# Attention visits ahead of an expert layer: sums inverted a visit sooner, transposes and copies issued ahead of exponents, other counts of constant products

## The chip, the cores and the metric

The kernel runs on one core of a Trainium2 chip. The metric is device time in microseconds (us), the median of the runs; 884.2 us for the kernel before, from three runs between 883.71 and 885.02. A lower time is better.

## The reference

Windowed attention over 8 batches, 8 heads, 576 positions and 64 elements a head, followed by an expert layer on all 4608 tokens.

```python
scores = scale * np.matmul(q, k.transpose(0, 1, 3, 2))
scores = np.where(masks[None, :, :, :], scores, -1000000000.0)   # 32 keys, or every 4th of 128
attn = np.exp(scores - np.max(scores, axis=-1, keepdims=True))
attn = attn / (np.sum(attn, axis=-1, keepdims=True) + 1e-09)
x = np.matmul(attn, v).transpose(0, 2, 1, 3).reshape(B * S, H * D)
h = x @ w_in                      # 4608 x 512 by 512 x 2048
sp = np.maximum(h, 0.0) + np.log1p(np.exp(-np.abs(h)))
out = (h * erf(sp)) @ w_out       # 2048 x 512
```

The weights come as double-precision words; the kernel makes of each a high and a low part on the chip.

## The kernel before

**Units and visits.** The attention is cut into 72 units of four blocks of 64 queries, for two heads at once. Unit n is begun at visit n and ended at visit n + 3 (LAG = 3). A visit is one pass of `first_visit(n)` (L366), of which the first 14 (FIRST = 14, n = 0 to 13) run ahead of the first product of the expert layer; later visits are woven into the steps of that layer (from L1342). Below, m = n - 3 is the unit that a visit ends.

**The steps of a unit**, with the engine and line of each: scores (TensorE, 32 small products, L224); the mask with the row maximum (VectorE, four instructions, L235); exponents with their row sums (ScalarE, four instructions, L245); 1e-9 added to the sums (POOL, L250); the reciprocal of the sums (VectorE, L257) and the multiplication of the probabilities by it (POOL, L258), together `normalize`; two transposes (TensorE, L263); a copy of the transposed probabilities from PSUM to SBUF, `turned` (L267, on ScalarE or VectorE); values (TensorE, 32 small products, L282); row copies out of PSUM (ScalarE, L324). When a pair of heads is complete, `finish` splits its rows into a high part (ScalarE, L329) and a low part (VectorE, `part_lo`, L335).

**The weights.** Visits 1 to 9 (EARLY = 9) also prepare weights: `prep_act` on ScalarE (L446 casts the high part of a tile made in the visit before, L451 begins the next tile), `prep_dve` on VectorE behind the visit (L460 the low part, L464 to L466 shift and combine the words of the tile that ScalarE began a visit earlier). At its end `prep_dve` issues the load of a further tile into the buffer that has come free (L431, 512 KB).

**The queues.** The order of instructions on every engine is the order in which the program issues them. All loads are issued on SP: q and k of unit n + 2 behind the scores of visit n (L208, 272 or 288 KB, two buffers, free when the scores two units before are done), v of unit n - 1 at the end of visit n (L212, 256 KB, two buffers, free when the values of unit n - 3 are done), and the weights tile at the end of `prep_dve`. So SP's order in a visit is q and k, v, weights.

**The visit before.** TensorE has transposes of m, scores of n, constant products, values of m, constant products. The constant products (`busy`, L364) multiply a constant tile into a PSUM bank that nobody reads until the first real product overwrites it; a visit that ends a unit has two behind the scores and two behind the values, the others six behind the scores. VectorE has `normalize(n - 2)`, then the mask of n, then the low parts, then the weights. ScalarE has the copy for unit m (visits 3 to 9; VectorE has it in visits 10 to 13), the weights, the row copies, the high part, the exponents of n. POOL has the multiplication for unit n - 2, then the addition for unit n. Behind the last visit `normalize(FIRST - 2)` follows, then the first step of the expert layer: transposes of unit 11 and the first product (L528).

Of the kernel before, what the change touches and what calls it, by code (L numbers as in the profile page):

```python
# [66 lines left out]
FIRST = NBLK + LAG + 2  # L67
# [3 lines left out]
EARLY = 9  # L71
# [75 lines left out]
def attn_moe_kernel(ctx: ExitStack, tc: tile.TileContext, qk, v, masks, eye, w_in, w_out, out):  # L147
    nc = tc.nc
# [47 lines left out]
    def turn_place(u):  # L196

        return (acc[(u + 1) % 4] if u < FREE else spb[u in second])[:, PARTS * P:2 * PARTS * P]
# [6 lines left out]
    def load_qk(u):  # L205
        if u < NU:
            n = QW + key_start(u, SPU - 1) + KEYS
            nc.sync.dma_start(out=qkz[u % 2][:, 0:n], in_=qk[u, :, 0:n])  # L208

    def load_v(u):  # L210
        if has(u):
            nc.sync.dma_start(out=vz[u % 2], in_=v[u].rearrange("p (s h d) -> p s h d", s=SIDE, h=2))  # L212
# [28 lines left out]
    def exponents(u):  # L241
        nmax = maxes.pop(u)
        sums[u] = small.tile([P, 2 * PARTS], F32, name="ssum", bufs=LAG + 1)
        for j in range(2 * PARTS):
            nc.scalar.activation(  # L245
                out=probs[u][:, j, :], in_=probs[u][:, j, :], func=AF.Exp,
                scale=-1.0, bias=nmax[:, j:j + 1], accum_out=sums[u][:, j:j + 1],
            )
        if u < FIRST:
            nc.gpsimd.tensor_scalar(sums[u], sums[u], 1.0e-9, None, op0=ALU.add)  # L250

    def normalize(u):
        rinv = small.tile([P, 2 * PARTS], F32, name="rinv")

        if u >= FIRST:
            nc.vector.tensor_scalar(sums[u], sums[u], 1.0e-9, None, op0=ALU.add)  # L256
        nc.vector.reciprocal(out=rinv, in_=sums.pop(u))  # L257
        nc.gpsimd.tensor_tensor(probs[u], probs[u], rinv.broadcast_to([P, 2 * PARTS, KEYS]), op=ALU.mult)  # L258

    def transposes(u):  # L260
        pr = probs.pop(u)
        for h in range(2):
            nc.tensor.transpose(out=turn_place(u)[:, h * P:(h + 1) * P],  # L263
                                in_=pr[:, PARTS * h:PARTS * (h + 1), :].rearrange("p a k -> p (a k)"), identity=ident)

    def turned(u, copy):
        copy(out=pz[u in second][:, 0:2 * P], in_=turn_place(u))  # L267
# [54 lines left out]
    def rows(u):  # L322
        for to, src in rows_of(u):
            nc.scalar.copy(out=to, in_=src)  # L324
# [7 lines left out]
    def part_lo():  # L332
        while halved:
            hi, lo, src = halved.pop(0)
            nc.vector.tensor_tensor(out=lo, in0=src, in1=hi.bitcast(F32), op=ALU.subtract)  # L335
# [20 lines left out]
    def has(u):  # L356
        return 0 <= u < NU
# [3 lines left out]
    def busy(k):  # L361

        for _ in range(k):
            nc.tensor.matmul(h, idle[:, 0:P], idle, start=True, stop=True)  # L364

    def first_visit(n):  # L366

        m = n - LAG
        copy = nc.scalar.copy if 1 <= n <= EARLY else nc.vector.tensor_copy
        if has(m):  # L370
            transposes(m)
        scores(n)
        load_qk(n + 2)
        busy(2 if has(m) else 6)
        if has(m):
            turned(m, copy)
        if 1 <= n <= EARLY:
            prep_act()
        if has(m):
            values(m)  # L380
            busy(2)
        if has(n - 2):
            normalize(n - 2)
        mask_max(n)
        part_lo()
        if has(m):
            rows(m)
            finish(m)
        if m == NBLK - 1:
            part_lo()  # L390
        exponents(n)
        load_v(n - 1)

# [920 lines left out]
    with tc.manual_schedule():  # L1314
# [6 lines left out]
        for n in range(FIRST):  # L1321
# [2 lines left out]
            first_visit(n)  # L1324
            if 1 <= n <= EARLY:
                prep_dve()
        normalize(FIRST - 2)
        part_lo()

        plan, late = visits()  # L1330
# [196 lines left out]
```

## Time and profile before

| what | value |
|---|---|
| median of three runs | 884.2 us |
| the profiled execution's own time | 884.02 us |
| its span, first to last instruction | 882.2 us |
| granted TensorE clock, mean | 0.998 |
| TensorE busy | 98% of the span |
| VectorE, ScalarE, POOL busy | 79%, 69%, 9% |
| first visit's scores start | 4.65 us |
| first product of the expert layer starts | 49.26 us |

The span is what the profile covers, 1.8 us less than the execution's own time. A row of a timeline tells when an instruction ran and, in brackets, how long its engine had been idle and what ended that. A share over the whole span is an average over stages: the first 49 us, which the diff touches, have other limits than the rest, where TensorE is busy nearly all the time. The granted clock is the share of full speed (2.4 GHz) at which TensorE was let run.

### The profile page before, as it was taken

What the parts mean: (1) busy time and instruction counts of PE and PEld (TensorE: products, weight loads), DVE (VectorE), ACT (ScalarE), POOL (GpSimd) and SP (SyncE); (2) the same over time, 40 slices, a digit from 0 to 9 for tenths busy, and PEclk for the clock granted to TensorE, in tenths of its full rate; (3) what the DMA queues carried; (4) which work ended last, traced back from release to release, by engine and by line L of the source; (5) the groups of instructions that cost most, each with busy time, mean ns of one, the idle gap of its engine ahead of it and who ended that gap; (6) DMA issues with size and microseconds to landing.
All of it is one profiled execution on the core that took longest, in us unless ns stands there. A gap on an engine that the chain in (4) does not pass through costs nothing.

```text
span 882.2 us, 21971 instructions
## 1 busy us (share of the span) xinstructions
PE 861.0 (98%) x8410; PEld 709.1 (80%) x8422; DVE 696.2 (79%) x1766; ACT 608.2 (69%) x1364; POOL 79.7 (9%) x97
## 2 busy tenths in 40 slices
PE   7689999999999999999999999999999999999998
PEld 3467888888888888888888888888888888889998
DVE  5888888987688889877766875667887968888985
ACT  6889888897797886675677652774656547785441
POOL 2312201111111100001000100000000000000000
PEclk9999999999999999999999999999999999999999
DMA  8874446474558797667576843674688449999332
GB/s 279 293 252 153 138 146 199 141 239 131 182 211 277 272 312 300 206 200 254 183 231 223 285 168 107 207 245 169 201 261 299 169 143 323 333 338 366 127 121 65
DMA packets 83161, 193.03 MB, mean 219 GB/s; under 512 B 9072, under 2 KB 25712, under 8 KB 79984
## 3 DMA queue, kind: packets, MB, share of 16 engines
q1 hardware_dynamic: 80096, 183.17, 61.6%
q10 hardware_dynamic: 2960, 8.46, 2.4%
q8 instruction: 66, 1.08, 0.5%
q14 instruction: 39, 0.32, 0.1%
HBM read 133.92 MB, written 57.67 MB: 217 GB/s over the span
## 4 chain that ended last, share of the span: by engine, by line
PE 90%; DMA 3%; ACT 3%; DVE 2%; issue 1%; POOL 0%; SPq 0%; DVEq 0%; POOLq 0%
PE acc L643 32%; PE h L803 10%; PE tx L803 10%; PE h L528 7%; PE tx L528 7%; PE sp L803 6%; PE acc L1166 4%; PE sp L282 3%; PE sp L224 3%; PE sp L1166 3%; PE sp L263 1%; DMA dbl<-in_w_in_dram 1%; PE tx L1166 1%; PE h L1166 1%; ACT prob L245 1%
## 5 line engine op out<-in xcount | busy, mean ns | idle before, releaser
L643 PE MATMUL acc<-wout_hi,ghi 128*128 128x512 f32 x448 | 177.4, 396 | 0.0
L643 PE MATMUL acc<-wout_lo,ghi 128*128 128x512 f32 x448 | 174.7, 390 | 0.0
L643 PE MATMUL acc<-wout_hi,glo 128*128 128x512 f32 x448 | 123.9, 390 | 0.2 <-DVE glo L619 0.2
L258 POOL TENSOR_TENSOR prob<-prob,rinv 128x256 f32<-128x256 f32 x72 | 71.5, 1001 | 473.2 <-DVE ssum L256 237.5
L245 ACT ACTIVATE prob<-prob,nmax 128x64 f32<-128x64 f32 x288 | 96.3, 338 | 10.5 <-DVE nmax L235 10.3
L643 PEld LDWEIGHTS acc<-wout_hi,glo 128*128 128x128 f32 x448 | 84.0, 188 | 18.4 <-DVE glo L619 0.6
L643 PEld LDWEIGHTS acc<-wout_hi,ghi 128*128 128x128 f32 x448 | 84.2, 188 | 17.0 <-DVE ghi L618 0.4
L643 PEld LDWEIGHTS acc<-wout_lo,ghi 128*128 128x128 f32 x448 | 84.2, 188 | 16.7
L235 DVE CUSTOM_DVE_ANT_0 prob<-sp,cst 128x64 f32<-128x64 f32 x288 | 45.2, 220 | 37.1 <-ACT rows L324 25.9
L852 ACT ACT_TABLE_LOAD x26 | 33.4, 1283 | 48.9 <-DVE hc L820 24.6
L803 PE MATMUL tx<-win 128*128 128x512 f32 x216 | 55.9, 394 | 0.0
L803 PE MATMUL h<-win 128*128 128x512 f32 x216 | 55.8, 394 | 0.0
L245 ACT ACTIVATION_READ_ACCUMULATOR prob<-prob,nmax 128x1 f32 x288 | 54.6, 190 | 0.0
L528 PE MATMUL h<-x,win 128*128 128x512 f32 x192 | 48.8, 396 | 0.0
L528 PE MATMUL tx<-x,win 128*128 128x512 f32 x192 | 48.0, 392 | 0.0
L803 PEld LDWEIGHTS h<-win 128*128 128x128 f32 x216 | 39.9, 188 | 9.3 <-DVE dbl L822 0.7
L803 PEld LDWEIGHTS tx<-win 128*128 128x128 f32 x216 | 39.9, 188 | 9.1 <-DVE hc L822 0.3
L324 ACT COPY rows<-sp 128x128 f32<-128x128 f32 (+7 forms) x167 | 27.5, 308 | 27.2 <-PE sp L224 26.8
L852 ACT ACTIVATE s<-dbl 128x1024 f32<-128x1024 f32 x22 | 23.3, 1061 | 27.4 <-DVE dbl L820 27.3
L528 PEld LDWEIGHTS h<-x,win 128*128 128x128 f32 x192 | 35.4, 188 | 8.0
L528 PEld LDWEIGHTS tx<-x,win 128*128 128x128 f32 x192 | 35.7, 188 | 7.5
L282 PEld LDWEIGHTS sp<-pT,v 64*64 64x64 f32 x1824 | 29.3, 134 | 10.6 <-DVE s L612 4.6
(338 smaller groups left out, 1938.5 us busy)
## 6 DMA issues: line engine op xcount, KB each, us to landing
win<-ws SPq DMA_DIRECT2D x24, 1024.0 KB, 5.3
v<-in_v_dram SPq DMA_DIRECT2D x72, 256.0 KB, 4.7
win<-ws SPq DMA_DIRECT2D x24, 768.0 KB, 6.0
qk<-in_qk_dram SPq DMA_DIRECT2D x48, 272.0 KB, 5.0
dbl<-in_w_in_dram SPq DMA_DIRECT2D x16, 512.0 KB, 4.4
dbl<-in_w_out_dram SPq DMA_DIRECT2D x16, 512.0 KB, 4.0
ws<-x SPq DMA_DIRECT2D x32, 256.0 KB, 4.3
win<-wd SPq DMA_DIRECT2D x14, 512.0 KB, 8.8
```

The source lines that it names most:

```text
L224: nc.tensor.matmul(sps[h][r * STRIP:(r + 1) * STRIP, i, p, :], qkz[i][hs, s * STRIP:(s + 1) * STRIP], qkz[i][hs, at:at + KEYS], start=True ...
L235: nc.vector.tensor_tensor_reduce(out=pr[:, g, :], in0=sps[h][:, u % 2, p, :], in1=mask[QUADS.index(kinds(u, p))], scale=-SCALE, scalar=HUG ...
L245: nc.scalar.activation(out=probs[u][:, j, :], in_=probs[u][:, j, :], func=AF.Exp, scale=-1.0, bias=nmax[:, j:j + 1], accum_out=sums[u][:, ...
L258: nc.gpsimd.tensor_tensor(probs[u], probs[u], rinv.broadcast_to([P, 2 * PARTS, KEYS]), op=ALU.mult)
L263: nc.tensor.transpose(out=turn_place(u)[:, h * P:(h + 1) * P], in_=pr[:, PARTS * h:PARTS * (h + 1), :].rearrange("p a k -> p (a k)"), iden ...
L282: nc.tensor.matmul(xp[h * D:(h + 1) * D, qs], vt[ks, s, h, :], pt[ks, h * P + s * STRIP:h * P + (s + 1) * STRIP], start=True, stop=True, t ...
L324: nc.scalar.copy(out=to, in_=src)
L528: nc.tensor.matmul((h, bank)[j], win_at[:, ftp, j, cc // 2, w, cc % 2, :], x[cc], start=(k == 0 and i == 0), stop=(k == CC - 1 and i == 2))
L643: nc.tensor.matmul(args["out"], args["lhsT"], args["rhs"], start=args["start"], stop=args["stop"])
L803: nc.tensor.matmul(bank_, w[:, wi, c, :], x[c][:, xi, :], start=(c == 0 and n == 0), stop=(c == 1 and n == 2))
L852: nc.scalar.activation(out=l, in_=e, func=AF.Softplus)
L1166: nc.tensor.matmul(y, x[:, at_], w, start=(q == 0 and j == 0 and n == 0), stop=(q == QUART - 1 and j == 1 and n == 2))
```

## The change

- `normalize` moves within the visit: for unit n - 1 behind the mask of n and the row copies, instead of for unit n - 2 ahead of the mask of n. On VectorE the reciprocal thereby stands ahead of the weights of the same visit. `normalize(FIRST - 2)` behind the last visit is dropped, as visit 13 contains it.
- The transposes of unit m + 1 and the copy of them stand at the end of visit n, ahead of the exponents of n, instead of at the head of visit n + 1. The first are in visit 2; visit 13 has none, as the first step of the expert layer transposes unit 11 as before. The copy is on ScalarE in visits 2 to 9 (units 0 to 7, one more than before) and on VectorE in visits 10 to 12 (units 8 to 10).
- Constant products: three behind the scores and three behind the values in visits 3 to 10, one and one in visits 11 to 13. Visits 0 to 2 keep their six.

```diff
--- before.py
+++ after.py
@@ -366,21 +366,14 @@
     def first_visit(n):
 
         m = n - LAG
-        copy = nc.scalar.copy if 1 <= n <= EARLY else nc.vector.tensor_copy
-        if has(m):
-            transposes(m)
         scores(n)
         load_qk(n + 2)
-        busy(2 if has(m) else 6)
-        if has(m):
-            turned(m, copy)
+        busy(6 if not has(m) else 3 if n <= EARLY + 1 else 1)
         if 1 <= n <= EARLY:
             prep_act()
         if has(m):
             values(m)
-            busy(2)
-        if has(n - 2):
-            normalize(n - 2)
+            busy(3 if n <= EARLY + 1 else 1)
         mask_max(n)
         part_lo()
         if has(m):
@@ -388,6 +381,11 @@
             finish(m)
         if m == NBLK - 1:
             part_lo()
+        if has(n - 1):
+            normalize(n - 1)
+        if has(m + 1) and n + 1 < FIRST:
+            transposes(m + 1)
+            turned(m + 1, nc.scalar.copy if n <= EARLY else nc.vector.tensor_copy)
         exponents(n)
         load_v(n - 1)
 
@@ -1324,7 +1322,6 @@
             first_visit(n)
             if 1 <= n <= EARLY:
                 prep_dve()
-        normalize(FIRST - 2)
         part_lo()
 
         plan, late = visits()
```

## Rows read from the trace of the kernel before

**Rows 1.** The page, part 1, for the whole span: busy us of each engine (share of the span) and x its instructions.

```profile
PE 861.0 (98%) x8410; PEld 709.1 (80%) x8422; DVE 696.2 (79%) x1766; ACT 608.2 (69%) x1364; POOL 79.7 (9%) x97
```

**Rows 2.** The chain of waits that ended last, in order of time: start us, us, what.

```profile
36.27 5.58 DMA v<-in_v_dram
...
45.00 0.42 DVE pT L267
...
45.79 0.22 POOL ssum L250
...
46.09 0.62 POOL prob L258
...
46.76 0.44 PE acc L263 x2
```

**Rows 3.** The timeline of TensorE (PE): start us, us, engine, line, operation, output<-inputs, x merged, and in brackets the idle time before it with what ended it. L263 are transposes, L364 constant products, L224 scores, L282 values, L528 the first products of the expert layer. Some records of L364 are missing.

```profile
11.62 0.38 PE L263 MATMUL acc<-ident,prob 128*128 128x128 f32 x2
...
25.89 1.04 PE L364 MATMUL h<-plain 128*128 128x512 bf16 x2
...
41.34 0.46 PE L224 MATMUL sp<-qk 64*32 64x64 f32 x32 [0.27 <-DMA qk<-in_qk_dram]
41.96 0.38 PE L364 MATMUL h<-plain 128*128 128x512 bf16 x1 [0.16 <-DMA v<-in_v_dram]
42.27 0.67 PE L282 MATMUL acc<-pT,v 64*64 64x32 f32 x32
42.87 0.60 PE L364 MATMUL h<-plain 128*128 128x512 bf16 x2
...
45.48 0.67 PE L282 MATMUL acc<-pT,v 64*64 64x32 f32 x32 [0.57 <-DVE pT L267]
...
49.09 0.41 PE L263 MATMUL acc<-ident,prob 128*128 128x128 f32 x2
49.26 3.02 PE L528 MATMUL h<-x,win 128*128 128x512 f32 x12
...
61.03 0.67 PE L282 MATMUL acc<-pT,v 64*64 64x32 f32 x32 [0.52 <-DMA v<-in_v_dram]
...
71.20 0.41 PE L263 MATMUL sp<-ident,prob 128*128 128x128 f32 x2 [1.13 <-DVE nmax L235]
```

**Rows 4.** The table of stretches: from:to in us, length, then busy us (x instructions) of TensorE, of its weight loads, of VectorE, ScalarE and POOL, the granted TensorE clock as a share of full speed, the busy share of the DMA engines, GB/s.

```profile
11.07:38.70 27.63, 19.28 (x522) 10.96 (x528) 25.63 (x98) 25.41 (x107) 8.23 (x14) 0.94 0.90 298
38.80:49.26 10.46, 8.23 (x244) 4.86 (x247) 5.51 (x43) 6.95 (x39) 3.86 (x8) 1.00 0.86 261
21.00:24.50 3.50, 1.56 (x36) 0.77 (x36) 3.28 (x14) 2.86 (x14) 0.15 (x1) 1.00 0.96 316
24.90:28.30 3.40, 3.07 (x69) 1.92 (x70) 2.52 (x8) 3.33 (x14) 1.94 (x4) 0.50 0.83 302
49.26:71.20 21.94, 19.45 (x324) 14.84 (x324) 20.26 (x65) 19.76 (x53) 5.74 (x9) 1.00 0.82 273
```

**Rows 5.** DMA issues of the v loads in four short windows, in order: the loads issued at 32.84 (unit 7), 36.27 (unit 8), 39.61 (unit 9) and 43.02 us (unit 10). Columns: output<-input, queue, operation, x issues, KB each, median us from issue to landing.

```profile
v<-in_v_dram SPq DMA_DIRECT2D x1, 256.0 KB, 4.3
...
v<-in_v_dram SPq DMA_DIRECT2D x1, 256.0 KB, 5.6
...
v<-in_v_dram SPq DMA_DIRECT2D x1, 256.0 KB, 4.8
...
v<-in_v_dram SPq DMA_DIRECT2D x1, 256.0 KB, 3.8
```

**Rows 6.** The timeline of VectorE (DVE), columns as in rows 3. L460 is the subtraction of a weights tile, L464 its shift, L465 and L466 its two combining steps, L267 the copy of transposed probabilities.

```profile
20.00 0.69 DVE L460 TENSOR_TENSOR win<-w,win 128x512 fp32r<-128x512 f32 x1
20.60 0.84 DVE L464 TENSOR_SCALAR w<-w 128x512 int32<-128x512 int32 x1
...
24.38 0.68 DVE L460 TENSOR_TENSOR win<-w,win 128x512 fp32r<-128x512 f32 x1
24.98 0.42 DVE L464 TENSOR_SCALAR w<-w 128x512 int32<-128x512 int32 x1
...
26.16 0.98 DVE L466 SCALAR_TENSOR_TENSOR w<-dbl,w 128x512 int32<-128x512 int32 x1
...
34.59 0.69 DVE L466 SCALAR_TENSOR_TENSOR w<-dbl,w 128x512 int32<-128x512 int32 x1
...
47.23 0.42 DVE L267 COPY pT<-acc 128x256 f32<-128x256 f32 x1 [1.18 <-PE acc L263]
```

**Rows 7.** The timeline of POOL, columns as in rows 3. L258 is the multiplication by the reciprocals, L250 the addition to the sums.

```profile
20.07 1.08 POOL L258 TENSOR_TENSOR prob<-prob,rinv 128x256 f32<-128x256 f32 x1
24.73 0.71 POOL L250 TENSOR_SCALAR ssum<-ssum 128x4 f32<-128x4 f32 x1 [3.58 <-ACT prob L245]
```

**Rows 8.** Groups of VectorE's instructions from 11 to 39 us: line, engine, operation, output<-inputs, shapes, x count | busy us, mean ns of one | idle us before them and what ended most of it. L235 is the mask with the row maximum.

```profile
L235 DVE CUSTOM_DVE_ANT_0 prob<-sp,cst 128x64 f32<-128x64 f32 x31 | 5.0, 216 | 1.4 <-PE sp L224 1.4
L464 DVE TENSOR_SCALAR w<-w 128x512 int32<-128x512 int32 x8 | 4.6, 578 | 0.0
```

**Rows 9.** The timeline of ScalarE (ACT), columns as in rows 3. L245 is the first exponent instruction of unit 2, L267 the copy of transposed probabilities of unit 0.

```profile
11.66 0.33 ACT L245 ACTIVATE prob<-prob,nmax 128x64 f32<-128x64 f32 x1
...
12.98 0.34 ACT L267 COPY pT<-acc 128x256 f32<-128x256 f32 x1
```

**Rows 10.** Who waited for whom on ScalarE from 11 to 39 us: the waiting line, what it waited for, us in total, times, longest us.

```profile
ACT w L451 <- DMA dbl<-in_w_in_dram: 3.2, 3, 1.5
```

## The prediction, made before the changed kernel was run

> **What bounds the kernel now.** I read the page first: TensorE is busy for 98% of the span [rows 1], so a time can change only where TensorE has nothing to do, or does something that the result doesn't need. The stretch that the diff touches is the start, before the first product of the expert layer. The chain of waits says what sets its end [rows 2]. To 42 us it runs through loads, the last of them v for unit 8, issued at 36.27 and landed 5.58 us later. From there it passes through the values of unit 8, its row copies and its split on ScalarE, the subtraction and the copy of unit 9 on VectorE, the two POOL steps and the transposes of unit 10. The first product starts at 49.26 [rows 3].
>
> The table by stage [rows 4] splits this. From 11.07 to 38.70 (visits 3 to 9, with weights, and the end of visit 2) VectorE is busy 25.63 of 27.63 us, ScalarE 25.41, the DMA engines 90% at 298 GB/s, TensorE 19.28: three resources near their limit, TensorE not one of them. From 38.80 to 49.26 (visits 10 to 13, no weights) none is: VectorE 5.51 of 10.46 us, ScalarE 6.95. There the chain is made of waits. Behind the first product TensorE is the bound, but for a few short waits, of 0.52 and 1.13 us among others [rows 3], which all hang on work that itself follows the first product: 19.45 of 21.94 us from 49.26 to 71.20 are busy [rows 4]. So I carry a shift of the first product to the end one to one.
>
> **Part by part.** TensorE's order hardly changes: the transposes of unit m+1 at the end of visit n stand where those at the head of visit n+1 stood, behind the same values and ahead of the same scores. What changes is who is ready for them, and the filling. No transfer moves on SP's queue; the two POOL steps change places.
>
> 1. *The inversion, one visit sooner.* The reciprocal and the POOL multiplication of unit n-1 now follow the mask of visit n. Today POOL does the addition for a unit first and then the multiplication for the unit before it: at 45.79 the addition for unit 11, at 46.09 the multiplication for unit 10, and the transposes at 46.76 [rows 2]. The multiplication will stand ahead of that addition, a visit earlier, and no transposes wait for it.
>
> 2. *The end of the stretch.* I replay it from the values of unit 8. Today they start at 42.27, behind scores at 41.34 and two constant products [rows 3]. With one product less, of 0.22 us (two show 0.60 to the end of the second, one 0.38), they start at 42.05; v has landed by then (36.27 + 5.58 = 41.85) [rows 2, 3]. From the values of unit 8 to those of unit 9 the links stay: row copies, split, subtraction and copy, from 42.27 to 45.48, 3.21 us [rows 3]; the reciprocal that now stands ahead of the copy adds some 0.1. That is 45.35. Then values (0.60 until the next products start) and one product: transposes of unit 10 at 46.17, today 46.76, held by POOL. The copy begins 0.47 us behind the transposes (46.76 and 47.23) and the values 0.48 behind the copy (45.00 and 45.48) [rows 2, 3, 6]: values of unit 10 at 47.1, or 47.2 with the scores and the product that stand ahead of them. Their v was issued at 43.02 behind the values of unit 8 and took 3.8 us [rows 5]; 0.2 sooner it lands at 46.6 and isn't waited for. Values 0.60, a product 0.22, and 0.17 from the transposes to the first product [rows 3]: 48.2 instead of 49.26. **Gain 1.1 us.** The VectorE copies of this stretch lie on that path, with 0.42 each, before and after.
>
> 3. *The middle, visits 2 to 10.* What matters is when v for unit 8 is issued. On SP it stands behind the weights load of visit 8, which waits for the end of visit 8's weights on VectorE, 34.59 + 0.69 [rows 6]. Four edits move that.
>  (a) *VectorE and POOL collide.* The multiplication took 0.62 us at 46.09 and 1.08 at 20.07, where VectorE had begun the subtraction of weights at 20.00; the shift at 20.60 then took 0.84, beside 0.42 at 24.98 [rows 2, 6, 7]. The shifts' mean of 578 ns over eight [rows 8] is that of three at 0.84 and five at 0.42; once the last combining step was hit (0.98 for 0.69) [rows 6]; otherwise the multiplication lay beside the mask. Issued directly ahead of the weights it falls on the shift each time: up to visit 8 seven times instead of three, 4 x 0.42 - 0.29 = +1.4 us. The other end is that it falls on none: -3 x 0.42 - 0.29 = -1.55.
>  The Trainium skill ("SBUF — State Buffer", section "Who interferes with whom") says that VectorE and GpSimd share one pair of ports, taken as a lock for a whole instruction by VectorE's two-port modes and, against a GpSimd operation that reads SBUF, by its instructions with two SBUF inputs. It speaks against this change, and the four long or late instructions here agree with it: by it the shift pays every time, the +1.4; without it, at today's mean for a shift, the term would be 0.
>  (b) *A new wait on VectorE.* The reciprocal of unit n-1 needs the exponents of visit n-1 and POOL's addition. Behind it on VectorE stand the weights, and behind those the next mask and SP's weights load. At 24.38, where the mask and the subtraction of visit 6 are done, the addition has yet to begin; it ends at 24.73 + 0.71 = 25.44: a wait of up to 1.06 [rows 6, 7]. In other visits the addition ends near the mask's end. Between 0 and 1.06 a visit, I take 0.85 in all.
>  (c) *Transposes and copies ahead of exponents.* Visit 2's copy now waits for transposes behind six constant products, which end at 12.00; with 0.34 for the copy its exponents start some 0.6 later than 11.66 [rows 3, 9]. ScalarE's waits for weights loads, 3.2 us in three [rows 10], absorb that. Later ScalarE comes to the copy behind row copies, when the transposes are done; if it came early it would wait for them, up to the two more products' 0.44. One copy goes from VectorE to ScalarE, behind the point that matters.
>  (d) *Waits that go.* VectorE's 1.4 us idle for scores [rows 8] go if scores come sooner.
>  Issue: 1.4 + 0.85 - 1.4 = 0.85 later. But the landing follows the load on the queue: v for unit 8 took 5.6 us, 4.3 and 4.8 its neighbours [rows 5]; a later issue meets a shorter queue, and I give back 0.75. **Loss 0.1 us**, with ends of 0.85 later and 0.75 sooner (no collision, half the wait).
>
> 4. *More constant products.* Visits 3 to 10 issue six instead of four, 16 x 0.22 = 3.5 us more; visits 11 to 13 two instead of four. TensorE's 19.28 of 27.63 us leave 8.3 idle [rows 4]: nothing, at full clock. The granted clock was half (1.2 of 2.4 GHz) from 24.9 to 28.3, behind a stretch with 1.56 us of products in 3.5, and two constant products then took 1.04 instead of 0.60 [rows 3, 4]. More filling may avoid that, or lengthen it by 2 x 0.44 a visit. Ends: -0.4 to +0.9; taken as 0, since ScalarE and VectorE, busy 3.33 and 2.52 of those 3.4 us, cover either.
>
> Sum against the profiled execution: 884.0 (span 882.2 and 1.8 around it) - 1.1 + 0.1 = **883.0 us**. The median of the runs shown is 0.2 higher, well inside the range.
>
> **Rivals.**
> *The middle gives as well* (faster). If the multiplication misses the shift, v for unit 8 is there 0.75 sooner: 883.0 - 0.85 = 882.1. At most the loads set the pace: 298 GB/s for 27.63 us and 261 for 10.46 are 10.96 MB; at the 316 GB/s of 21.0 to 24.5 [rows 4] they take 34.7 instead of 38.1 us. So 3.4 us are the limit, 880.6. For it: three resources each idle a little, and a chain that now hangs on loads alone. Against: the collision shows wherever the two follow each other. Chance of a gain over 1.8 us (0.2%, about what a measurement of this kernel can tell from no change): 0.35.
> *The new wait paces the visits* (slower). Place: the reciprocal on VectorE, ahead of the weights. At 0.5 us in each of seven visits it costs 3.5; with the collisions' 1.4, less the 1.4 idle, everything behind visit 8 comes 3.5 later, and 1.1 comes back at the end: 886.4. It outweighs the gain from some 0.25 us a visit, where 7 waits less the 0.75 of a shorter queue reach 1.1. For it: VectorE has only 2.0 us idle in the stretch [rows 4]. Against: the additions mostly end no later than the mask. Chance 0.17.
> *The loads hide everything* (no change). If each landing moves back by what its issue gains, v for unit 8 stays at 41.9, and loads of q and k pace the scores behind it, as they did at 41.34 [rows 3]: 884.0. With my forecast 0.48.
> *A half clock nearer the first product.* Fewer products in visits 11 to 13 could bring the fall there; one visit's scores, values, products and transposes, 0.46 + 0.60 + 0.44 + 0.41 [rows 3], would take as much again: 884.9. It lies in the range.
>
> **How the numbers follow.** Same (within 0.2%) 0.48, faster 0.35, slower 0.17. The range of 881.0 to 885.5 leaves out the last part of the load limit below and the new wait at full price above.
>
> **What would show it.** Right: transposes of units 9 to 11 no longer wait for POOL; the first product between 47.5 and 49; shifts of 0.84 in most visits; reciprocals with an idle VectorE of some tenths ahead of them. Wrong: v for unit 8 landed well before 41 or after 43; the shift at 0.42 throughout; the clock's fall moved to 40 or later; waits behind the first product that grow by what it gained.

## The result and the profile after

The changed kernel is slower: a median of 888.73 us (886.57 to 890.72, 6 executions) beside 884.11 (883.03 to 885.02, 6) for the kernel before, ratio 1.0053 with a 95% interval of [1.0037, 1.0069]. 883.0 was forecast, with a range of 881.0 to 885.5; the time lies outside it. The profiled execution took 888.56 us, with a span of 886.8, 4.6 more than before.

TensorE's timeline of the kernel after, around the end of the first stretch (start us, us, engine, line, operation, x merged, in brackets the idle time before it with what ended it; L224 scores, L263 transposes, L282 values, L364 constant products, L526 first products):

```profile
29.88 0.68 PE L224 MATMUL sp<-qk 64*32 64x64 f32 x32 [1.87 <-DMA qk<-in_qk_dram]
...
41.85 0.67 PE L282 MATMUL acc<-pT,v 64*64 64x32 f32 x32 [0.45 <-DVE pT L267]
42.46 0.39 PE L364 MATMUL h<-plain 128*128 128x512 bf16 x1
42.68 0.38 PE L263 MATMUL acc<-ident,prob 128*128 128x128 f32 x2
44.30 0.46 PE L224 MATMUL sp<-qk 64*32 64x64 f32 x32 [1.24 <-DMA qk<-in_qk_dram]
45.49 0.67 PE L282 MATMUL acc<-pT,v 64*64 64x32 f32 x32 [0.73 <-DVE nmax L235]
46.09 0.39 PE L364 MATMUL h<-plain 128*128 128x512 bf16 x1
46.32 0.38 PE L263 MATMUL acc<-ident,prob 128*128 128x128 f32 x2
47.55 0.80 PE L224 MATMUL sp<-qk 64*32 64x64 f32 x32 [0.85 <-DMA qk<-in_qk_dram]
48.82 1.08 PE L282 MATMUL acc<-pT,v 64*64 64x32 f32 x32 [0.47 <-DVE nmax L235]
49.83 0.61 PE L364 MATMUL h<-plain 128*128 128x512 bf16 x1
50.23 0.64 PE L263 MATMUL acc<-ident,prob 128*128 128x128 f32 x2
50.52 4.45 PE L526 MATMUL h<-x,win 128*128 128x512 f32 x12
```

Beside [rows 3]: the values of unit 8 start at 41.85, 0.42 us sooner than before and 0.2 sooner than the forecast's 42.05. Up to there the change has lost nothing. From there to the first product the kernel before needed 6.99 us, the forecast gave 6.15, and now it is 8.67: two waits for q and k, of 1.24 and 0.85, and from 47.55 on scores of 0.80 instead of 0.45 and values of 1.08 instead of 0.67. The first 12 products take 4.45 instead of 3.02. By the first product of the second layer (74.04 us, before 71.37) the kernel is 2.67 late, 1.26 of it from the later start and 1.43 from the slow products. Much of the 1.26 is the clock's as well. The scores of unit 13 started before at

```profile
47.12 0.45 PE L224 MATMUL sp<-qk 64*32 64x64 f32 x32
```

and now start at 47.55, 0.43 later. The other 0.83 lies behind them, where the granted clock was half. So of the 2.67 us some 2.3 arose at half clock in this execution, behind waits that by themselves had cost 0.43 against the kernel before.

The end of the chain of waits of the kernel after (start us, us, what) no longer runs through v, the row copies, VectorE's copy and POOL as in [rows 2]. It hangs on q and k twice:

```profile
24.66 5.08 DMA qk<-in_qk_dram
...
41.55 5.86 DMA qk<-in_qk_dram
...
50.87 4.10 PE h L526 x12
```

Stretches of the kernel after (columns as in [rows 4]):

```profile
11.07:38.70 27.63, 21.78 (x529) 12.85 (x538) 24.58 (x93) 23.54 (x100) 8.25 (x14) 0.88 0.87 289
...
27.00:30.00 3.00, 1.13 (x19) 0.61 (x24) 2.97 (x13) 2.11 (x9) 1.67 (x2) 0.96 0.74 219
30.00:33.00 3.00, 2.67 (x67) 1.66 (x68) 2.93 (x14) 2.52 (x11) 0.22 (x1) 0.50 1.05 337
...
39.00:42.00 3.00, 2.55 (x81) 1.59 (x82) 2.85 (x18) 3.00 (x21) 1.10 (x2) 1.00 0.78 231
42.00:45.00 3.00, 1.52 (x67) 1.13 (x65) 1.46 (x10) 2.55 (x13) 0.57 (x3) 1.00 1.03 378
45.00:48.00 3.00, 1.66 (x66) 1.36 (x67) 1.24 (x11) 1.97 (x12) 1.35 (x3) 0.80 0.77 230
48.00:51.00 3.00, 2.53 (x56) 2.13 (x39) 0.86 (x10) 1.07 (x7) 0.83 (x2) 0.50 0.51 163
```

Two stretches of the kernel before, which were not read ahead of the forecast:

```profile
39.00:42.00 3.00, 2.00 (x69) 1.17 (x67) 1.72 (x11) 1.87 (x12) 1.69 (x4) 1.00 0.99 334
42.00:45.00 3.00, 2.53 (x70) 1.39 (x70) 1.24 (x9) 2.00 (x9) 0.50 (x1) 1.00 0.91 284
```

The same transfers moved: before, the DMA engines carry 334 GB/s from 39 to 42 us and 284 after that; now 231 and then 378, at a busy share of 1.03. They have room first and are then full, while TensorE waits for them. The granted clock falls twice, once behind 27 to 30 us, in which TensorE was busy for 1.13 us of 3.00, and once within 42 to 48 us, with 3.18 busy of 6.00; the second fall now covers the first products.

Why the loads bunch stands on SP's queue. Its timeline (start us, us, queue, line, load), first of the kernel before:

```profile
38.54 0.33 SPq L431 DMA_DIRECT2D dbl<-in_w_out_dram  x1
38.96 0.38 SPq L208 DMA_DIRECT2D qk<-in_qk_dram  x1
39.61 0.33 SPq L212 DMA_DIRECT2D v<-in_v_dram  x1
41.94 0.33 SPq L208 DMA_DIRECT2D qk<-in_qk_dram  x1
```

and of the kernel after:

```profile
40.03 0.33 SPq L429 DMA_DIRECT2D dbl<-in_w_out_dram  x1
40.45 0.38 SPq L208 DMA_DIRECT2D qk<-in_qk_dram  x1
40.93 0.38 SPq L212 DMA_DIRECT2D v<-in_v_dram  x1
41.55 0.33 SPq L208 DMA_DIRECT2D qk<-in_qk_dram  x1
```

The weights load of visit 9 waits for the end of visit 9's weights on VectorE, now 1.49 us later, and q and k of unit 12 stand behind it: they are issued 1.49 later too, at 40.45, though the scores of visit 10, behind which they are called for, end at 38.70. The same four loads are issued in 1.5 us instead of 3.4, and the last of them, q and k of unit 13, took longer to land. Its row in the DMA issues (KB each, us to landing), before:

```profile
qk<-in_qk_dram SPq DMA_DIRECT2D x1, 288.0 KB, 4.2
```

and after:

```profile
qk<-in_qk_dram SPq DMA_DIRECT2D x1, 288.0 KB, 5.9
```

VectorE's timeline of the kernel after shows why visit 9's weights end later (L257 reciprocal, L458 subtraction, L462 shift):

```profile
17.22 0.18 DVE L257 RECIPROCAL rinv<-ssum 128x4 f32<-128x4 f32 x1 [0.88 <-POOL ssum L250]
...
36.99 0.18 DVE L257 RECIPROCAL rinv<-ssum 128x4 f32<-128x4 f32 x1 [0.56 <-POOL ssum L250]
37.09 0.66 DVE L458 TENSOR_TENSOR win<-w,win 128x512 fp32r<-128x512 f32 x1
37.66 0.84 DVE L462 TENSOR_SCALAR w<-w 128x512 int32<-128x512 int32 x1
```

In visit 9 the reciprocal waits 0.56 for POOL's addition and the shift takes 0.84 beside POOL's multiplication. Before, the multiplication of that visit lay beside the subtraction:

```profile
35.84 0.84 DVE L460 TENSOR_TENSOR win<-w,win 128x512 fp32r<-128x512 f32 x1
36.60 0.41 DVE L464 TENSOR_SCALAR w<-w 128x512 int32<-128x512 int32 x1
```

The group of shifts from 11 to 40 us, beside [rows 8]:

```profile
L462 DVE TENSOR_SCALAR w<-w 128x512 int32<-128x512 int32 x7 | 5.4, 773 | 0.0
```

And the waits from 11 to 51 us (line, for what: us in total, times, longest):

```profile
PE sp L224 <- DMA qk<-in_qk_dram: 6.5, 6, 1.9
...
DVE rinv L257 <- POOL ssum L250: 2.3, 5, 0.9
```

Before, scores waited 1.3 us for q and k in the same stretch, and reciprocals not at all for POOL's addition.

Behind the second layer's first product the span is another 2.0 us longer (812.8 against 810.8). Over the 20 profiled executions here that remainder is 811.3 on the mean, from 809.8 to 813.1, with no tie to that start (correlation 0.05), and the spans follow the start of the second layer at 1.03 us for each us. So the start is carried to the end, and the remainder is scatter that the change cannot be charged with from one profile. The three largest waits of TensorE behind 75 us in the kernel after are for VectorE in a late stage (L1164), 1.1, 0.9 and 0.5 us; before, there was one of 0.9 on the same line.

The second execution of this kernel that was profiled (e5 below) reached its first product at nearly the same time, 50.49, in another way. Its four loads were issued within 2.79 us, from 41.11 to 43.90, the last landed after 4.6 us, and in visits 11 to 13 scores waited for q and k once, for 0.34 us. Its granted clock was down earlier (0.72 from 39 to 42 and 0.71 from 42 to 45), and the first products took 3.00:

```profile
48.61 0.67 PE L224 MATMUL sp<-qk 64*32 64x64 f32 x32
...
50.49 3.00 PE L526 MATMUL h<-x,win 128*128 128x512 f32 x12
```

So the bunch of loads and the slow first products describe the first profiled execution; they are not what every execution of this kernel loses by.

### The profile page after: what moved, and what is told of

Its sections match the earlier page's. It is cut to its first block, busy times and chain, and to the rows that moved or that the text cites. A ratio compares the mean times of both kernels' runs of the same rounds, so it can differ in the third digit from the quotient of the medians.

```text
span 886.8 us, 21986 instructions
## 1 busy us (share of the span) xinstructions
PE 866.5 (98%) x8420; PEld 713.7 (80%) x8432; DVE 697.1 (79%) x1765; ACT 608.6 (69%) x1365; POOL 79.6 (9%) x97
## 3 DMA queue, kind: packets, MB, share of 16 engines
q8 instruction: 66, 1.08, 0.5%
## 4 chain that ended last, share of the span: by engine, by line
PE 88%; DMA 4%; DVE 4%; ACT 2%; issue 1%; POOL 0%; SPq 0%; DVEq 0%; ACTq 0%; POOLq 0%
PE acc L641 33%; PE h L801 9%; PE tx L801 9%; PE h L526 7%; PE tx L526 7%; PE sp L801 5%; PE sp L282 3%; PE sp L224 3%; PE acc L1164 3%; PE sp L1164 2%; PE h L364 2%; PE sp L263 1%; DMA qk<-in_qk_dram 1%; DMA w<-ga 1%; DMA v<-in_v_dram 1%
## 5 line engine op out<-in xcount | busy, mean ns | idle before, releaser
L258 POOL TENSOR_TENSOR prob<-prob,rinv 128x256 f32<-128x256 f32 x72 | 71.3, 997 | 483.5 <-DVE ssum L256 236.9
L245 ACT ACTIVATE prob<-prob,nmax 128x64 f32<-128x64 f32 x288 | 96.4, 339 | 10.9 <-DVE nmax L235 10.7
L235 DVE CUSTOM_DVE_ANT_0 prob<-sp,cst 128x64 f32<-128x64 f32 x288 | 45.4, 220 | 36.0 <-ACT rows L324 26.0
L245 ACT ACTIVATION_READ_ACCUMULATOR prob<-prob,nmax 128x1 f32 x288 | 54.9, 191 | 0.0
L526 PE MATMUL h<-x,win 128*128 128x512 f32 x192 | 50.2, 404 | 0.0
L526 PE MATMUL tx<-x,win 128*128 128x512 f32 x192 | 48.0, 392 | 0.0
L526 PEld LDWEIGHTS h<-x,win 128*128 128x128 f32 x192 | 36.5, 194 | 8.4
L526 PEld LDWEIGHTS tx<-x,win 128*128 128x128 f32 x192 | 35.7, 188 | 7.5
L224 PE MATMUL sp<-qk 64*32 64x64 f32 x2304 | 32.8, 228 | 6.5 <-DMA qk<-in_qk_dram 6.5
```

The lines of the kernel that those rows point to most:

```text
L224: nc.tensor.matmul(sps[h][r * STRIP:(r + 1) * STRIP, i, p, :], qkz[i][hs, s * STRIP:(s + 1) * STRIP], qkz[i][hs, at:at + KEYS], start=True ...
L235: nc.vector.tensor_tensor_reduce(out=pr[:, g, :], in0=sps[h][:, u % 2, p, :], in1=mask[QUADS.index(kinds(u, p))], scale=-SCALE, scalar=HUG ...
L245: nc.scalar.activation(out=probs[u][:, j, :], in_=probs[u][:, j, :], func=AF.Exp, scale=-1.0, bias=nmax[:, j:j + 1], accum_out=sums[u][:, ...
L526: nc.tensor.matmul((h, bank)[j], win_at[:, ftp, j, cc // 2, w, cc % 2, :], x[cc], start=(k == 0 and i == 0), stop=(k == CC - 1 and i == 2))
```

## The experiments

Each of the 18 kernels was executed 12 times beside 23 or 35 executions of the kernel before on the same chip. The medians of the kernel before were 884.88 to 885.56. "Difference" is that of the means, in us. The last three columns are of the one profiled execution, which is one draw: its time can lie almost 4 us from the median, so the verdicts go by the ratio. The ratio is not the quotient of the two means: e1 and e3 have the same difference and ratios of 1.0010 and 1.0022. Half a microsecond between two rows says nothing. "First" is the start of the first product (with the time of its 12 products), "second" that of the second layer.

| kernel | median us | difference | ratio [95%] | profiled us | first (12 products) | second |
|---|---|---|---|---|---|---|
| before | | | | 884.02 | 49.26 (3.02) | 71.37 |
| after, first comparison | 888.73 | +4.66 | 1.0053 [1.0037, 1.0069] | 888.56 | 50.52 (4.45) | 74.04 |
| after, again (e5) | 888.30 | +2.50 | 1.0024 [1.0004, 1.0044] | 886.30 | 50.49 (3.00) | 72.58 |
| e1 new order, old products | 885.87 | +1.05 | 1.0010 [0.9997, 1.0023] | 887.04 | 52.13 (3.02) | 74.23 |
| e2 old order, new products | 885.76 | +0.84 | 1.0010 [0.9995, 1.0025] | 887.92 | 50.88 (3.04) | 73.00 |
| e3 new order, three throughout | 886.08 | +1.05 | 1.0022 [1.0013, 1.0031] | 883.95 | 49.78 (3.02) | 71.88 |
| e6 old order, three throughout | 884.77 | -0.32 | 0.9999 [0.9986, 1.0012] | 884.29 | 50.41 (2.99) | 72.49 |
| e4 after, inversion behind weights | 887.81 | +1.92 | 1.0025 [1.0013, 1.0037] | 888.35 | 52.41 (3.00) | 74.49 |
| e8 inversion alone | 884.86 | -0.32 | 1.0000 [0.9988, 1.0012] | 884.31 | 50.01 (2.98) | 72.08 |
| e9 transposes and copies alone | 887.53 | +1.99 | 1.0019 [1.0005, 1.0033] | 885.87 | 52.23 (3.03) | 74.35 |
| e16 after, copy behind exponents | 886.78 | +1.53 | 1.0019 [1.0003, 1.0035] | 886.45 | 50.78 (4.26) | 74.12 |
| e7 new order, fewer in tail only | 886.57 | +1.59 | 1.0024 [1.0009, 1.0038] | 890.35 | 52.58 (4.49) | 76.15 |
| e10 new order, none in tail | 885.23 | +0.69 | 1.0005 [0.9992, 1.0017] | 887.93 | 51.01 (5.39) | 75.48 |
| e11 old order, none in tail | 886.13 | +1.21 | 1.0013 [1.0000, 1.0026] | 885.52 | 49.50 (4.06) | 72.63 |
| e12 after, loads held | 885.39 | +0.04 | 1.0000 [0.9985, 1.0015] | 883.02 | 47.61 (3.02) | 69.58 |
| e13 before, loads held | 883.88 | -0.92 | 0.9986 [0.9976, 0.9997] | 883.86 | 48.70 (3.02) | 70.81 |
| e14 e3 with loads held | 885.19 | -0.04 | 1.0001 [0.9989, 1.0014] | 885.06 | 48.89 (2.98) | 70.95 |
| e15 e8 with loads held | 884.26 | -0.87 | 0.9989 [0.9978, 0.9999] | 883.33 | 47.88 (3.02) | 70.00 |
| e17 e15, three throughout | 884.46 | -0.51 | 0.9994 [0.9981, 1.0007] | 884.95 | 50.25 (3.02) | 72.36 |
| e18 before, weights load behind q, k | 885.09 | +0.72 | 1.0007 [0.9992, 1.0022] | 887.97 | 52.60 (3.02) | 74.70 |

**Order or products?** *e1*: the new order with the old constant products.

```diff
-        busy(6 if not has(m) else 3 if n <= EARLY + 1 else 1)
+        busy(2 if has(m) else 6)
...
-            busy(3 if n <= EARLY + 1 else 1)
+            busy(2)
```

> The changed kernel with the constant products of before (two and two in visits 3 to 13); only the order is new. Clock theory (one and one products in visits 11 to 13 let the clock fall ahead of the first product): no half clock at the first product, its twelve products take 3.0 us instead of 4.45, the time comes back to 884 to 885.5. Order theory (the reciprocal ahead of the weights lengthens VectorE's visits, q and k come late and TensorE starves): the fall stays and the time stays at 887.5 to 889.

*e2*: the reverse diff, in the kernel before.

> The kernel before with the constant products of the change (three and three in visits 3 to 10, one and one in 11 to 13); the order is the old one. Clock theory: the fall comes here too, 886 to 888. Order theory: no change, 883.5 to 884.8.

*e3*: the change with three products at both places in every visit.

```diff
-        busy(6 if not has(m) else 3 if n <= EARLY + 1 else 1)
+        busy(6 if not has(m) else 3)
...
-            busy(3 if n <= EARLY + 1 else 1)
+            busy(3)
```

> The changed kernel with three and three constant products in visits 11 to 13 as well. Clock theory: full clock at the first product, 885.5 to 886.5 (2.5 us off, 0.6 back for the longer visits). Order theory: no gain, 888 to 889.5.

*e6*: the same in the kernel before.

> The kernel before with three and three constant products in visits 3 to 13. Clock theory: no fall, as TensorE is never idle for long; the time is that of before or up to 1 us lower. The rival, that more constant products lengthen the visits: 1 to 2 us slower than before, since e3 with the same products stood 0.9 above it.

*e5*: the change itself once more, beside the same executions of the kernel before as e6.

> The changed kernel itself, beside the kernel before in more rounds. Both theories: slower by 3 to 5 us; the granted clock is at half for the last stretch ahead of the first product in this profile too. If it comes within 1.5 us of the kernel before, most of the first difference was scatter between executions.

What follows: with three products throughout, the clock stayed at full speed in the profile of e3 and the first 12 products took 3.02, yet the new order still cost 1.05 us, against -0.32 for e6. So the clock is not the whole cause. The granted clock that is on record for every execution says the same. Its mean over the 12 executions is 0.9986 in e3 and 0.9989 in e6, 0.9941 in e5, and 0.9953 in the kernel before beside e5 and e6. Within the executions of one kernel a clock lower by 0.001 goes with 0.29 us more (385 executions, correlation -0.46; in e5 alone 0.70 us), so the 0.0012 that e5 lies under the kernel before is worth, by estimate, 0.3 to 0.8 us of its 2.50. Neither half alone shows a loss beyond its interval of the ratio (e1, e2); together (e5) they do. The split between them is within these intervals and stays open. The change was repeated at +2.50, smaller than the first +4.66; both are slower.

**Which move?** *e8*: in the kernel before, only the inversion moved, to behind the row copies (the one behind the last visit is dropped, as in the change). *e9*: only `transposes` and `turned` moved.

```diff
-        if has(n - 2):
-            normalize(n - 2)
...
+        if has(n - 1):
+            normalize(n - 1)
         exponents(n)
```

> Only the inversion moved (unit n-1 behind the mask of n, ahead of the weights); transposes, copies and products as before. Order theory: the wait for POOL's additions and the collisions at the shift come with it, 1 to 2 us slower than before. If the inversion is harmless and the copy ahead of the exponents is what costs: within 0.7 us of before.

```diff
-        if has(m):
-            transposes(m)
...
-        if has(m):
-            turned(m, copy)
...
+        if has(m + 1) and n + 1 < FIRST:
+            transposes(m + 1)
+            turned(m + 1, nc.scalar.copy if n <= EARLY else nc.vector.tensor_copy)
         exponents(n)
```

> Only the transposes and copies moved to the end of the visit, ahead of the exponents; inversion and constant products as before. If the copy ahead of the exponents is what costs in the new order (e1 stood 0.7 to 1.0 above before, e8, the inversion alone, at before): 1 to 3 us slower, as the transposes now wait for a multiplication of the same visit and ScalarE for the transposes. If the order is harmless and the tail's products are all: within 0.5 us of before.

*e4*: the change, with the inversion behind the weights of its visit.

```diff
-        if has(n - 1):
-            normalize(n - 1)
...
             if 1 <= n <= EARLY:
                 prep_dve()
+            if has(n - 1):
+                normalize(n - 1)
```

> The changed kernel with the inversion of unit n-1 behind the weights of visit n instead of ahead of them; transposes, copies and products as changed. Order theory: VectorE no longer waits for POOL's additions (2.3 us in all) and the shifts lose part of their collisions, q and k come sooner: 885 to 886.5. Clock theory: the fall ahead of the first product remains, 887.5 to 889.

*e16*: the change, with the copies behind the exponents again.

```diff
-            turned(m + 1, nc.scalar.copy if n <= EARLY else nc.vector.tensor_copy)
         exponents(n)
+        if has(m + 1) and n + 1 < FIRST:
+            turned(m + 1, nc.scalar.copy if n <= EARLY else nc.vector.tensor_copy)
```

> The changed kernel with the copy of the transposed probabilities behind the exponents again; inversion, transposes, products as changed. If ScalarE's wait for the transposes ahead of the exponents is the cost: 1 to 2 us below the change, within 1.2 us of before. If the cost is in the products and the loads: as the change, 2.5 us above before.

What follows: the inversion alone shows no cost (-0.32), though it brings the collision (six shifts of 0.83 or 0.84 in e8). The transposes and copies alone cost 1.99. In e9 ScalarE, which did not wait for transposes before, does, from 11 to 51 us (two rows of e9's waits):

```profile
PE acc L263 <- POOL prob L258: 6.8, 5, 2.0
...
ACT pT L267 <- PE acc L263: 4.2, 6, 1.2
```

The first row is why: the transposes stand where POOL's multiplication for their unit is not yet done, and TensorE waits 6.8 us for it (before 1.0, e4 7.7, and no such wait in the kernel after).

The waits of that stretch and the issue of the last weights load, side by side:

| kernel | ScalarE's copy for transposes, us | reciprocal for POOL's addition | scores for q, k | last weights load |
|---|---|---|---|---|
| before | 0 | 0 | 1.3 | 38.54 |
| after | 0.6 | 2.3 | 6.5 | 40.03 |
| e5, after again | 1.9 | 1.8 | 3.6 | 41.11 |
| e8 inversion alone | 0 | 0.7 | 1.4 | 40.22 |
| e9 transposes and copies alone | 4.2 | 0 | 0 | 40.28 |
| e4 inversion behind weights | 5.5 | 0 | 0 | 41.56 |
| e16 copy behind exponents | 0 | 0.2 | 0.9 | 38.73 |
| e3 three throughout | 0.3 | 0.6 | 1.7 | 38.84 |

The two moves belong together: without the earlier inversion the transposes and copies wait (e9, e4). That the copies, standing ahead of the exponents, delay the sums for which the reciprocal waits fits after and e5 (2.3 and 1.8) against e8 and e16 (0.7 and 0.2), but is not shown: with the copies in the new place e3 has 0.6, and with the copies in the old place e15, further below, has 1.1. With the copy put back (e16) both waits are all but gone and the last weights load is issued 0.19 later than before; still its mean loses 1.53, not clearly less than e5's 2.50, with executions from 883 to 891. e16 keeps the change's products, which alone went with +0.84 (e2), so its loss need not come from the moves. Nor does a late weights load alone cost time: e8 issues it at 40.22, later than the kernel after, and loses nothing. So the waits are explained in part, and the time less.

**The clock in the tail.** *e7*: the new order with 2+2 products up to visit 10 and 1+1 behind it; *e10*: none behind it; *e11*: the same in the old order. The edit of e10 (e7 has 1 in place of each 0):

```diff
-        busy(6 if not has(m) else 3 if n <= EARLY + 1 else 1)
+        busy(6 if not has(m) else 2 if n <= EARLY + 1 else 0)
...
-            busy(3 if n <= EARLY + 1 else 1)
+            busy(2 if n <= EARLY + 1 else 0)
```

> The changed order, two and two products in visits 3 to 10 as before, one and one in visits 11 to 13 as changed. Clock theory with the tail as the place: half clock at the first product as in the change, 2 to 3.5 us slower than before. If the place is the middle (three and three in visits 3 to 10): like e1, within 1 us of before.

> The changed order, two and two constant products in visits 3 to 10, none in visits 11 to 13. Clock theory with the tail as the place: half clock at the first product in all executions, 3 to 5 us above before, more than e7 (1.0 to 1.6 above). Load theory (q, k and v pace the tail and the clock matters little): no more than e1 or e7, 1 us above.

> The old order, two and two constant products in visits 3 to 10, none in visits 11 to 13. Clock theory: the fall comes here as well, 2 to 4 us above before. If the old order keeps TensorE busy enough by spreading its waits, and only the new order's single wait a visit lets the clock fall: within 1 us of before, with a clock near that of before.

What follows: without products in the tail the first 12 products took 5.39 us (e10) and 4.06 (e11), with one and one 4.49 (e7). The mean granted clock over their 12 executions is 0.9901, 0.9905 and 0.9896, against 0.9940 in e1, with two and two, and 0.9953 to 0.9957 in the kernel before beside them. So the tail's products do keep the clock up. But e10 lost 0.69 us, e11 1.21 and e7 1.59, about as much as e3, whose first products ran at full clock (1.05). Slow first products can be a part of the loss; they do not decide it.

**The loads.** *e12*: the change, with the weights loads of visits 8 and 9 kept back until visit 12 is issued, so that q, k and v of the tail stand ahead of them.

```diff
+            if n == EARLY - 1:
+                hold(True)
             first_visit(n)
+            if n == FIRST - 2:
+                hold(False)
```

> The changed kernel, but the two weights loads of visits 8 and 9, which no instruction ahead of the first product needs, are issued behind visit 12. Load theory: q, k and v of the last units no longer queue behind 1 MB of weights, the waits for q and k in visits 11 to 13 (1.2 and 0.9 us) go, and with them the fall of the clock: 2 to 4 us faster than the change, at or below before. Clock theory without the loads: the change's time within 1 us.

SP's timeline in e12:

```profile
41.35 0.33 SPq L208 DMA_DIRECT2D qk<-in_qk_dram  x1
...
43.27 0.33 SPq L208 DMA_DIRECT2D qk<-in_qk_dram  x1
...
45.98 1.92 SPq L429 DMA_DIRECT2D dbl<-in_w_out_dram  x2
```

TensorE's timeline in e12:

```profile
42.67 0.45 PE L224 MATMUL sp<-qk 64*32 64x64 f32 x32
44.80 0.67 PE L282 MATMUL acc<-pT,v 64*64 64x32 f32 x32 [1.68 <-DVE pT L267]
...
45.94 0.45 PE L224 MATMUL sp<-qk 64*32 64x64 f32 x32
46.65 0.67 PE L282 MATMUL acc<-pT,v 64*64 64x32 f32 x32 [0.25 <-DVE pT L267]
...
47.61 3.02 PE L526 MATMUL h<-x,win 128*128 128x512 f32 x12
```

and the stretch from 39 to 42 us:

```profile
39.00:42.00 3.00, 2.39 (x89) 1.65 (x82) 2.79 (x20) 2.64 (x18) 1.48 (x3) 1.00 0.43 152
```

The scores of visits 11 to 13 no longer wait for q and k (the last such wait is 0.47 us at 32.95), the DMA engines are at 0.43 instead of 0.78, the clock does not fall and the first product starts 2.9 us sooner than in the kernel after. The loss of the change goes from +2.50 (e5) to +0.04; the interval of e12 overlaps a little with that of e5 and not with that of the first comparison. (This profiled execution lies 2.4 us under e12's median, so the 47.61 is a good draw.) The same edit was made in three other kernels: *e13*, the kernel before; *e14*, e3; *e15*, e8.

> The kernel before with the two weights loads of visits 8 and 9 issued behind visit 12. Load theory: q, k and v of the last units come sooner here too, 1 to 2.5 us faster than before. Theory that only the new order needs them sooner (the old one waits for POOL and VectorE instead): within 0.7 us of before.

> The changed order with three and three products in all visits 3 to 13 and the two weights loads held back. If the clock ahead of the first product matters once the loads don't bind: 0.5 to 1.5 us faster than e12, 1 us below before. If not: like e12, at before.

> The inversion alone moved, two and two products, the two weights loads held back. If the moved transposes and copies are what costs in the change: the fastest of these four, 1.5 to 3 us below before. If they help once the loads don't bind: slower than e14.

The mean fell in all four, by 2.5, 0.9, 1.1 and 0.55 us; the smallest, e15 against e8, lies within the intervals, and the others are at their edge or just beyond it. With the loads out of the way the new order still gains nothing over the old one (e12 +0.04, e14 -0.04; e13 -0.92, e15 -0.87). The lowest are e13, the kernel before with the loads held, at 0.9986 [0.9976, 0.9997], and e15 at 0.9989. So part of what e12 gains, 0.9 of 2.5, is there for the kernel before too; with the loads held in both, the change is still 0.96 slower (e12 against e13), which is within the intervals.

*e17* puts the parts that cost nothing together: e15 with three products at both places.

> The earlier inversion, three and three constant products in visits 3 to 13, the old places of transposes and copies, the two weights loads of visits 8 and 9 held back behind visit 12. If the parts add: 1 to 1.5 us below before. If the products lengthen the shorter tail: no better than e13 and e15, 0.5 to 0.9 below.

It is no better than e13.

*e18*: the kernel before, with each visit's weights load issued behind the next visit's q and k.

```diff
         load_qk(n + 2)
+        hold(False)
...
             if 1 <= n <= EARLY:
+                hold(True)
                 prep_dve()
```

> The kernel before with each weights load of visits 1 to 9 issued behind the q and k load of the next visit, so that q and k never wait on SP for VectorE; the same bytes. If SP's order was the cost: 0.7 to 1.5 us below before, as e13. If it was the bytes ahead of q, k and v: no gain, or a loss up to 1 us, as the weights come later.

It gave nothing. In the old order q and k hardly wait for the weights load, so this does not say whether, in the change, it is the place on SP's queue or the 0.5 MB of bytes that make q and k late. e12 takes away both.

## Why the prediction was wrong, step by step

*Step 1* held: up to the first product no row of the kernel after has transposes waiting for POOL (behind it one does, 1.43 us at 65.61).

*Step 2* failed. Its first link held (values of unit 8 at 41.85 for 42.05). It then replayed the tail with every other load landing as before, and looked at v for unit 10 alone. q and k of units 12 and 13 were late, by waits of 1.24 and 0.85 us, and the half clock that followed stretched the rest: 8.67 us in place of 6.15. A first product as early as the forecast's 48.2 appears in two profiles only, both with the loads held (47.61 in e12, 47.88 in e15), and both are single draws. The mean times there gain 0.9 at most, and e13 gains it without the change. In e5's profile the tail went wrong in another way: its q and k were all but in time, while half clock, and waits of 0.84 and 0.93 us for the copies of units 7 and 9, held TensorE, and the first product came at 50.49 as well.

*Step 3, (a)*: right as rows; six of the seven shifts in the group took 0.83 or 0.84. The rule cited there from the Trainium skill ("SBUF — State Buffer", "Who interferes with whom") agrees again: visit 9's shift took 0.84 beside the multiplication, and 0.41 before, where the multiplication lay beside the subtraction. *(b)*: the kind was right, the size was not: 2.3 us in five waits, up to 0.88; 1.5 of it falls into the visits up to 8, for which 0.85 was taken. Its working looked at the additions as they stood, and not at what (c) may do to them. e8, with the collisions and 0.7 us of waits, loses nothing; e16, with 0.2 of waits, loses: neither row has a price of its own that the runs confirm. *(c)* was taken as absorbed; without the inversion it costs 1.99 (e9), and that it makes (b) larger is argued, not shown. *(d)*: VectorE's waits for scores fell from 1.4 to 0.5 us, not to nothing.

The step that failed inside 3 is its last one. It followed the weights load of visit 8 and v behind it, found 0.85 later, and gave 0.75 back, since "a later issue meets a shorter queue". In the profile that load was 0.58 later and v behind it 1.15, and v, which landed after 3.8 us instead of 5.6, did meet a shorter queue. The load that was left out is visit 9's, 1.49 later. Behind it the queue was not shorter but bunched: the q and k at its end took 5.9 us instead of 4.2. So what failed in steps 2 and 3 is the same assumption, that behind v for unit 8 every load lands as before. What the runs show in its place is that most of the loss hangs on the weights loads ahead of the tail's q, k and v: with the two loads held the change is at +0.04 instead of +2.50, and 0.96 above the kernel before with the same loads held. By which waits they do so differs from execution to execution (e5), and the bunch by itself is no loss: in e8 the four loads went out within 2.28 us, the last took 5.1, and the time did not rise.

*Step 4* took the products as free, with +0.9 as one end. The half clock, one fall of 3.4 us before, became two falls, and the second lay on the first products: 1.43 us in the profiled execution. The rival of a half clock nearer the first product came true in that execution as an event. But e5's profiled execution ran its first products in 3.00 us, and was still slower than before.

Of the rivals, "the loads hide everything" had the right resource and the wrong sign: the loads did not only keep the gain, they took more. "The new wait paces the visits", at a chance of 0.17, had the right sign and 886.4 us, but not by its own mechanism: at 1.5 us in seven visits the waits are below the 0.25 a visit from which it was to outweigh the gain, and the values of unit 8 came sooner, not 3.5 us later. None of the four had what happened.

What stays open: how the loss divides between the order and the products; why e16 still loses 1.5 us where the waits of the copies are gone, by the place of the transposes or by the products that it keeps; why the first comparison showed 4.66 and the second 2.50; by which waits the held loads save their 2.5 us in most executions; and what, in the late stage, makes TensorE wait 2.5 us for VectorE where before it was 0.9 on the same line.

## What to carry to other kernels

When a step is moved ahead of an engine's work that a load waits for, follow the last such load, not a typical one, and list what stands behind it on the queue: the stretch in which no other work is left can pay for the delay. A load that is not needed for long should not stand ahead of loads that the next visit needs: holding two of them back took 0.9 us off the kernel before, where the reordering added 2.5; letting each stand behind the q and k of one visit alone gave nothing (e18). And where the executions of one kernel lie 5 us apart from lowest to highest, as here, a profile is read for its order and its waits, and the gain from many executions. Two profiles of the same kernel, as here of the kernel after, tell which of its waits come back.

## What was not expected of the hardware

Loads on one queue can be late by being close together: four loads issued within 1.5 us instead of 3.4 ran the DMA engines at 378 GB/s, and the last landed after 5.9 us instead of 4.2. Over the 14 profiles in which visit 9's weights load, q and k, v, and q and k are issued in this order, the last takes on the whole longer the closer the four were issued: 3.5 us where they spread over 4.67 (e9), 5.1 over 2.28 (e8), 5.9 over 1.52. The correlation is -0.80; e7 (6.2 over 2.33) and e10 (4.2 over 2.43) show how loose it is.

Two stretches with nearly the same busy time went on differently. In the kernel after, with 1.52 us busy of 3.00 from 42 to 45, the granted clock fell within the next 3 us. In e12, whose row of the same stretch shows still less, it stayed at full speed:

```profile
42.00:45.00 3.00, 1.32 (x64) 0.97 (x60) 1.41 (x8) 2.63 (x12) 0.44 (x2) 1.00 0.80 217
```

There TensorE was busy for 2.75 of the 3.00 us that came next, against 1.66 in the kernel after.
